# Batch 0's units reordered (tokens 0-255 first), and the mixing probabilities loaded later, in a retention + mixture-of-experts kernel

## The chip, the cores and the metric

The kernel runs on one core of one Trainium2 chip. The metric is device time in microseconds (us) of one execution. The profiled span is some 1.7 us shorter than the device time of the same execution. Runs that were sent together share one chip and one set of runs of the kernel before; sets 2 to 5 ran on four different chips (that of set 1 isn't on record), which turned out to matter.

## The reference, cut to what matters

```python
scores = scale * np.matmul(q, k.transpose(0, 1, 3, 2))        # B, H, S, D = 8, 8, 576, 64
ret    = scores * Dmat                                        # causal decay gamma_h ** (i - j)
attn   = np.matmul(ret, v)
x      = attn.transpose(0, 2, 1, 3).reshape(B * S, H * D)     # 4608 tokens x 512
p = domain_probs / (domain_probs.sum(-1, keepdims=True) + 1e-9)
for e in range(4):
    h = np.maximum(x @ w1[e], 0.0)                            # 512 -> 1024, "up"
    out += p[:, e:e + 1] * (h @ w2[e])                        # 1024 -> 512, "down"
```

Of the kernel before, what the change touches and what calls it, by code (L numbers as in the profile page):

```python
# [23 lines left out]
def kernel(  # L24
# [10 lines left out]
    nc = tc.nc  # L35
# [12 lines left out]
    NT = 512  # L48
# [50 lines left out]
    def load_w1(e, f=slice(0, F)):  # L99
        return nc.gpsimd.dma_start(out=w1_sb[e][:, :, f], in_=moe_w1[e][:, f].rearrange("(dc p) f -> p dc f", p=128))  # L100

    def load_w2(e):
        return nc.gpsimd.dma_start(
            out=wx[e // 2][:, (e % 2) * NFC:(e % 2 + 1) * NFC, :, :].rearrange("p a b c -> p a (b c)"),
            in_=moe_w2[e].rearrange("(fc p) d -> p fc d", p=128))
# [9 lines left out]
    def load_unit(raw, b, hf, g, eng):  # L115
        for n, src in srcs:
            eng.dma_start(out=raw[n],
                          in_=src[b, 4 * g:4 * g + 4, 2 * C * hf:2 * C * hf + 2 * C, :]
                          .rearrange("h (p r) d -> p h (r d)", r=2))

    units0 = ((0, 0), (1, 0), (0, 1), (1, 1))
    p0 = const.tile([128, NT // 128, E], FP32, name="p0")
    prb = tpool.tile([128, N // 128, E], FP32, tag="p1", name="prb")
    for u, (hf, g) in enumerate(units0):
        load_unit({n: raw0[u][n][:, :, :, :].rearrange("p h r d -> p h (r d)") for n in "kqv"}, 0, hf, g, nc.sync)
    nc.sync.dma_start(out=p0, in_=moe_domain_probs[0:NT, :].rearrange("(g p) e -> p g e", p=128))
    nc.sync.dma_start(out=prb, in_=moe_domain_probs.rearrange("(p t) e -> p t e", p=128))


    zz = epool.tile([128, 512], BF16)  # L130
# [41 lines left out]
    def later_tables():  # L172
        nc.gpsimd.memset(tri, 1.0)
        nc.gpsimd.affine_select(out=tri, in_=tri, compare_op=mybir.AluOpType.is_ge, fill=0.0,
                                base=0, channel_multiplier=-1, pattern=[[1, C]])
        nc.gpsimd.tensor_copy(trir[0:R], tri[0:R, 0:R])
        nc.gpsimd.tensor_copy(trir[R:2 * R], tri[R:2 * R, R:2 * R])
        nc.gpsimd.iota(pos_j[:, 0:NC], pattern=[[C, NC]], base=0, channel_multiplier=1,
                       allow_small_or_imprecise_dtypes=True)
        for j in range(2):  # L180
            nc.gpsimd.iota(pos_j[64 * j:64 * j + 64, NC:NC + 1], pattern=[[0, 1]], base=SM, channel_multiplier=1,
                           allow_small_or_imprecise_dtypes=True)
        for n in "kqv":
            nc.gpsimd.memset(rawr[n], 0.0)
# [23 lines left out]
    def mixing_weights():  # L208
        nc.vector.tensor_reduce(psm, prb, axis=mybir.AxisListType.X, op=ADD)
        nc.vector.tensor_scalar_add(psm, psm, 1e-9)  # L210
        nc.vector.reciprocal(psm, psm)
        nc.vector.tensor_tensor(pn, prb[:, :, :].rearrange("p t e -> p e t"),
                                psm.unsqueeze(1).to_broadcast([128, E, NTT]), op=MULT)
        nc.sync.dma_start(out=pd[:, :].rearrange("e (p t) -> p e t", p=128), in_=pn)
# [467 lines left out]
        if u + 1 < NU:  # L682
            us[u + 1].kv()
    part.matmuls(1)
    mixing_weights()
    early.close()
    hp = ctx.enter_context(tc.tile_pool(name="hp", bufs=1))
    h = hp.tile([128, E * NFC, NT], BF16, name="h")
# [25 lines left out]
        load_unit({n: raws[u][n].rearrange("p (h x) -> p h x", h=4) for n in "kqv"}, 1, vs[u].hf, vs[u].g, nc.gpsimd)  # L714

    load_w2(0)
    load_w1(1)
    later_tables()
    load_w2(1)
    load_rem(0, nc.gpsimd)  # L720
# [8 lines left out]
    def remainder(slots, b, at):  # L729
        add = lambda i, f: slots.setdefault(i, []).append(f)  # L730
        x = Rem(b)
        l, c, tr, s, o = at
        if b > 0:
            add(l, lambda: load_rem(b))
        add(c, lambda: x.cast(nc.vector))
        add(tr, x.trans_pe)
        add(s, x.scores)
        add(o, x.values)
# [4 lines left out]

    slots = {}
    add = lambda i, f: slots.setdefault(i, []).append(f)
    add(0, mixing_weights0)
    add(1, later_decays)
    remainder(slots, 0, (-1, 13, 15, 16, 17))

    def v_cast(u):  # L750
# [49 lines left out]
    for b in range(2, B):  # L800
        g = NS * (b - 3)
# [72 lines left out]
```

## The kernel before: what the change touches

The expert layer works on tiles of 512 tokens. Tile 0 can start when batch 0's attention is there, so batch 0 has a code of its own, the prologue here. It works in four units, each 256 tokens (`hf`) of four heads (`g`). Each unit is loaded, scaled and cast, transposed, and turned into scores, key-value state and values:

```python
units0 = ((0, 0), (1, 0), (0, 1), (1, 1))                     # (hf, g)
for u, (hf, g) in enumerate(units0):
    load_unit(..., 0, hf, g, nc.sync)                         # k, q, v: 256 KB each, SP queue
nc.sync.dma_start(out=p0, ...)                                # small table: tile 0's probabilities, 512 pieces of 16 B
nc.sync.dma_start(out=prb, ...)                               # large table: all of them, 72 KB
# ... casts; load_w1(0) in two halves after the casts of units 1 and 2, on the software queue ...
for u in range(NU):
    if u + 2 < NU:
        cast_unit(u + 2)
    if u == NU - 1:
        part = UpHalf(0)                                      # early up projection: tokens 0-255, half of expert 0
        part.matmuls(0)
    us[u].values_own()
    if u + 1 < NU:
        us[u + 1].scores()
    us[u].values_carried()                                    # 2 matmuls for hf 0, 4 for hf 1
    if u + 2 < NU:
        us[u + 2].trans_pe(1)
    if u + 1 < NU:
        us[u + 1].kv()                                        # 8 matmuls for hf 0, 12 for hf 1
part.matmuls(1)
mixing_weights()                                              # normalise prb, write it to DRAM
```

Behind it the weights are loaded on the software queue, and tile 0 goes through the experts. The calls in `slots` are run between its matmul groups:

```python
load_w2(0); load_w1(1); later_tables(); load_w2(1); ...       # 1 MB each, fp32 cast to bf16 on the way
slots: 0 mixing_weights0 (normalise p0), 1 later_decays, ...
for e in range(E):
    for i in range(4):
        if e > 0 or i > 1: up_group(h, 0, e, i)
        run(slots, n); n += 1
    for m in range(4):
        down_plain(h, 0, e, m); run(slots, n); n += 1         # the first reads load_w2(0)'s weights
```

PSUM is a ring of four buffers. `down_plain` fills one for two groups of 128 tokens, and VectorE scales it with the normalised probabilities.

## Time and profile before

| | kernel before |
|---|---|
| device time, median of the first 3 runs | 535.76 us (535.12 to 537.06) |
| TensorE busy | 526.5 us, 99% of the span |
| TensorE idle, 5-20 us | 1.29 us |
| early up projection starts | 18.09 us |
| first down weights land | 25.83 us |
| first down matmul starts | 25.95 us |

A row of the timeline has the start, the length, engine, line, operation, operands and count, and in brackets how long the engine was idle before and what ended it. A row of DMA issues has the size and the time from issue to landing. The lines are in the prediction below.

How to read the first down matmul: matmuls of 128x512 follow each other at a pitch of 0.216 us, and the up group before has 16 of them. So the first down matmul is due 16 x 0.216 = 3.46 us after that group's first one. What it comes later, it has waited.

### The profile page before, as it was taken

The page shows a single profiled execution, that of the slowest core. Times are in us where ns is not written, and L with a number is a line of the kernel's source. Part 1 is how long each engine was busy: PE and PEld are TensorE (multiplying, and loading weights), DVE is VectorE, ACT ScalarE, POOL GpSimd, SP SyncE. Part 2 cuts the span into 40 slices and gives each one's busy share as a digit, 9 for nine tenths or more (in the row PEclk, how much of TensorE's full clock was granted, in tenths as well). Part 3 has the DMA queues.
Part 4 walks back from the last instruction along what each step waited for, and adds up shares of the span by engine and source line. Part 5 has one row for each costly group of instructions (what it writes and reads, how often), then busy time and mean ns, then how long its engine had stood idle before and what let it go on. Part 6 is the DMA issues. An engine that isn't in the chain of part 4 may idle for free.

```text
span 533.7 us, 10229 instructions
## 1 busy us (share of the span) xinstructions
PE 526.5 (99%) x4260; PEld 342.4 (64%) x4260; DVE 361.7 (68%) x456; ACT 86.0 (16%) x175; POOL 144.5 (27%) x187
## 2 busy tenths in 40 slices
PE   8999999999999999999999999999999999999997
PEld 4644544478745885478646865587548844884486
DVE  6426668895577767697578767777765567557763
ACT  4723450012101121020101001100110000000010
POOL 5734104236235334335132603153000000000000
PEclk9999999999999999999999999999999999999999
DMA  9999947877879967937353655454010111110001
GB/s 240 205 213 250 239 114 190 165 156 168 143 168 166 174 138 145 158 81 167 101 135 95 152 134 112 107 120 124 20 41 21 60 39 41 41 41 20 1 21 60
DMA packets 145118, 63.55 MB, mean 119 GB/s; under 512 B 124240, under 2 KB 135888, under 8 KB 145072
## 3 DMA queue, kind: packets, MB, share of 16 engines
q1 hardware_dynamic: 134752, 43.50, 38.2%
q0 software_dynamic: 10176, 19.27, 16.4%
q8 instruction: 33, 0.54, 0.4%
q10 hardware_dynamic: 144, 0.13, 0.1%
q14 instruction: 13, 0.11, 0.1%
HBM read 53.56 MB, written 9.51 MB: 118 GB/s over the span
## 4 chain that ended last, share of the span: by engine, by line
PE 73%; ACT 2%; DVE 0%; issue 0%
PE ph L359 37%; PE pd L471 34%; ACT xt L292 2%; PE o L284 1%; PE o L279 1%; PE py L471 1%; DVE h L365 0%; PE sr L338 0%; PE or L344 0%; PE or L346 0%; DVE ob L499 0%
## 5 line engine op out<-in xcount | busy, mean ns | idle before, releaser
L359 PE MATMUL ph<-xt,w 128*128 128x512 bf16 x1136 | 251.0, 379 | 0.8 <-DVE h L365 0.2
L365 DVE SCALAR_TENSOR_TENSOR h<-ph,pB 128x1024 bf16<-128x1024 f32 x128 | 156.5, 1224 | 58.7 <-PE ph L359 58.0
L359 PEld LDWEIGHTS <-w 128*128 128x128 bf16 x1136 | 109.9, 98 | 127.9
L471 PEld LDWEIGHTS <-h 128*128 128x128 bf16 x1024 | 100.0, 98 | 13.3
L471 PEld LDWEIGHTS <-s 128*128 128x128 bf16 x768 | 75.0, 98 | 8.7
L471 PE MATMUL pd<-wx,h 128*128 128x256 bf16 x512 | 61.1, 273 | 0.2
L471 PE MATMUL pd<-wx,s 128*128 128x256 bf16 x512 | 61.1, 273 | 0.0
L220 POOL DMA_DIRECT2D pB<-pd x28 | 15.8, 565 | 150.9 <-DVE h L365 131.8
L506 POOL TENSOR_TENSOR ob<-v,p 128x256 f32<-128x256 f32 x15 | 11.3, 755 | 114.0 <-DVE v L503 92.5
L239 POOL TENSOR_TENSOR bf_k<-raw_k,gk 128x512 bf16<-128x512 f32 x24 | 25.8, 1073 | 35.3 <-DMA raw_k<-in_k_dram 17.4
L271 DVE TENSOR_TENSOR sT<-s,tri 128x1024 bf16<-128x1024 f32 x24 | 28.3, 1219 | 6.4 <-PE s L269 6.4
L292 ACT ACTIVATE xt<-o 128x768 bf16<-128x768 f32 (+6 forms) x24 | 13.0, 594 | 116.8 <-PE o L284 116.8
L444 DVE TENSOR_TENSOR s<-s,h 128x1024 bf16<-128x1024 bf16 x32 | 31.2, 1013 | 0.0
L471 PE MATMUL pd<-t4w,h 128*128 128x256 bf16 x256 | 30.6, 273 | 0.0
L394 PE MATMUL po<-wx,h 128*128 128x512 bf16 x128 | 29.1, 379 | 0.1
L471 PE MATMUL pd<-t3w,h 128*128 128x256 bf16 x240 | 28.7, 273 | 0.0
L471 PE MATMUL pd<-t2w,s 128*128 128x256 bf16 x240 | 28.6, 273 | 0.0
L479 ACT ACTIVATE p<-pd 128x256 f32<-128x256 f32 x16 | 6.1, 384 | 138.8 <-PE pd L471 106.2
L239 POOL TENSOR_TENSOR bf_q<-raw_q,gq 128x512 bf16<-128x512 f32 x24 | 26.9, 1120 | 3.3 <-DMA raw_q<-in_q_dram 3.1
L442 DVE TENSOR_TENSOR s<-h 128x1024 bf16<-128x1024 bf16 x32 | 24.8, 816 | 0.0
L448 DVE TENSOR_TENSOR s<-h,s 128x1024 bf16<-128x1024 bf16 x32 | 24.7, 811 | 0.0
L488 DVE TENSOR_TENSOR u<-pd,p 128x256 f32<-128x256 f32 x15 | 6.4, 425 | 22.5 <-PE pd L471 22.5
(158 smaller groups left out, 375.2 us busy)
## 6 DMA issues: line engine op xcount, KB each, us to landing
pB<-pd POOLq DMA_DIRECT2D x28, 256.0 KB, 3.7
raw_k<-in_k_dram SPq DMA_DIRECT2D x48, 128.0 KB, 2.8
raw_q<-in_q_dram SPq DMA_DIRECT2D x48, 128.0 KB, 3.0
raw_v<-in_v_dram SPq DMA_DIRECT2D x48, 128.0 KB, 3.0
wx<-in_moe_w_dram POOLq DMA_DIRECT2D x4, 1024.0 KB, 15.4
out_dram<-oa SPq DMA_DIRECT2D x16, 256.0 KB, 2.2
out_dram<-ob SPq DMA_DIRECT2D x15, 256.0 KB, 2.2
w<-in_moe_w_dram POOLq DMA_DIRECT2D x3, 1024.0 KB, 15.1
```

Of the source, the lines that this page charges most:

```text
L220: eng.dma_start(out=pB[t, e], in_=pd[e:e + 1, t * NT:(t + 1) * NT].to_broadcast([128, NT]))
L239: eng.tensor_tensor(bfs[p % 2][n], raw1[n], g[:, :, 2 * p:2 * p + 2].unsqueeze(3).to_broadcast([128, NC, 2, D]), op=MULT)
L271: nc.vector.tensor_tensor(sT[:, :, :, :].rearrange("p j c t -> p (j c) t"), s[:, :, :, :].rearrange("p j c t -> p (j c) t"), tri[:, :].uns ...
L292: nc.scalar.activation(xt_of(t)[:, self.ps, n0 + a - t * NT:n0 + z - t * NT], o[:, :, a:z], Copy)
L359: nc.tensor.matmul(ph[:, f, :], lhsT=w1_sb[e][:, dc, fc * 128:(fc + 1) * 128], rhs=x[:, dc, :], start=(dc == 0), stop=(dc == NDC - 1))
L365: nc.vector.scalar_tensor_tensor(h[:, fk:fk + 2, :], ph, 0.0, pB[t, e][:, :].unsqueeze(1).to_broadcast([128, 2, NT]), op0=MAX, op1=MULT)
L394: nc.tensor.matmul(po[:, g, :], lhsT=h[:, e * NFC + fc, ns * 128:(ns + 1) * 128], rhs=wx[e // 2][:, (e % 2) * NFC + fc, :, :].rearrange("p ...
L442: nc.vector.tensor_tensor(self.alloc("s1")[:, l], h[:, l, self.b], h[:, r, self.b], op=ADD)
L444: nc.vector.tensor_tensor(self.alloc("s2")[:, l], self.s1[:, l], h[:, l, self.a], op=SUB)
L448: nc.vector.tensor_tensor(self.alloc("s4")[:, l], h[:, r, self.a], self.s2[:, l], op=SUB)
L471: mm = nc.tensor.matmul(dst, lhsT=src[:, kk, tok], rhs=rhs(c), start=(start and c == 0), stop=(c == KH - 1), skip_group_check=True)
L506: nc.gpsimd.tensor_tensor(self.ob[:, HF:Dm], self.v, self.p5, op=ADD)
```

## The change

It has two aims: to let tokens 0-255 be done for all heads first, since the early up projection needs only those; and to keep the probability loads and their normalisation out of the stretch in which the first weights are loaded.

```diff
-    units0 = ((0, 0), (1, 0), (0, 1), (1, 1))
+    units0 = ((0, 0), (0, 1), (1, 0), (1, 1))
...
-    nc.sync.dma_start(out=p0, in_=moe_domain_probs[0:NT, :].rearrange("(g p) e -> p g e", p=128))
-    nc.sync.dma_start(out=prb, in_=moe_domain_probs.rearrange("(p t) e -> p t e", p=128))
...
     part.matmuls(1)
-    mixing_weights()
...
     load_w2(0)
+    nc.gpsimd.dma_start(out=p0, in_=moe_domain_probs[0:NT, :].rearrange("(g p) e -> p g e", p=128))
     load_w1(1)
+    nc.gpsimd.dma_start(out=prb, in_=moe_domain_probs.rearrange("(p t) e -> p t e", p=128))
...
-    add(0, mixing_weights0)
-    add(1, later_decays)
+    add(0, later_decays)
+    add(3, mixing_weights0)
+    add(9, mixing_weights)
```

## The prediction

> **What bounds the kernel now.** I read the page first: the busy shares, then the slices.
>
> ```profile
> span 533.7 us, 10229 instructions
> PE 526.5 (99%) x4260; PEld 342.4 (64%) x4260; DVE 361.7 (68%) x456; ACT 86.0 (16%) x175; POOL 144.5 (27%) x187
> ...
> DMA  9999947877879967937353655454010111110001
> ```
>
> TensorE is busy from the first slice to the last, so the end can only move if TensorE's program gets shorter or has fewer gaps. All of the change lies in the first 40 us (batch 0's attention, called the prologue here, and tile 0 of the expert layer), and there the DMA row is at 9 as well. Next I asked for the busy time by stretch, with the columns stretch, its length, PE busy, PEld, DVE, ACT, POOL, granted clock, DMA share, GB/s:
>
> ```profile
> 5.00:10.00 5.00, 4.57 (x48) 2.49 (x47) 2.95 (x4) 1.50 (x2) 1.50 (x3) 1.00 1.11 297
> 10.00:15.00 5.00, 4.64 (x104) 3.48 (x104) 4.65 (x7) 4.17 (x10) 2.51 (x5) 1.00 1.24 260
> 15.00:20.00 5.00, 4.50 (x88) 3.31 (x86) 3.47 (x9) 3.49 (x9) 4.62 (x13) 1.00 1.28 208
> 20.00:25.00 5.00, 5.00 (x36) 3.31 (x34) 1.56 (x19) 4.11 (x9) 3.82 (x6) 1.00 1.22 203
> 25.00:30.00 5.00, 4.94 (x24) 2.08 (x22) 0.40 (x1) 1.33 (x2) 0.77 (x1) 1.00 1.14 203
> ```
>
> Between 5 and 20 us PE is idle for 0.43 + 0.36 + 0.50 = 1.29 us in all, and afterwards hardly at all. This caps what can be won by filling gaps at something over 1 us of 534, far under 2%. The filler matmuls on a zero tile (20, of some 0.38 us) stay in the program where they are, so they can't be won. Then I read the timeline from 15 us to 26 us for what holds PE in the places the change touches (start, length, engine, line, operation, count, idle before it and its releaser):
>
> ```profile
> 16.08 0.76 ACT L598 ACTIVATE sbd<-kvp 64x256 bf16<-64x256 f32 x2
> ...
> 16.89 0.28 PE L623 MATMUL o<-qkT,sbd 128*128 128x128 bf16 x2 [0.24 <-ACT sbd L598]
> ...
> 17.01 1.15 PE L578 MATMUL kvp<-bf_v,bf_k 128*128 128x256 bf16 x12
> 17.21 0.77 ACT L639 ACTIVATE xt<-o 128x256 bf16<-128x256 f32 x2 [0.38 <-PE o L623]
> ...
> 18.09 1.05 PE L380 MATMUL ph<-xt,w 128*128 128x256 bf16 x8
> ...
> 22.27 3.62 PE L359 MATMUL ph<-xt,w 128*128 128x512 bf16 x16
> ...
> 25.91 6.60 PEld L394 LDWEIGHTS <-h 128*128 128x128 bf16 x32 [0.52 <-issue]
> ```
>
> L380 is the early up projection over tokens 0-255. It needs the third unit's xt, which ACT finishes at 17.21 + 0.77 = 17.98, and PE reaches it at 18.09 anyway because the key-value products before it run until then. L394 is the first down projection: its weight loads stood idle for 0.52 us, put down to "issue". The list of instructions says that this load also waits for a DMA of the software queue, the first down weights (wx). The DMA view for the moment of their issue at 14.93 us says:
>
> ```profile
> wx<-in_moe_w_dram POOLq DMA_DIRECT2D x1, 1024.0 KB, 10.9
> ```
>
> They land at 14.93 + 10.9 = 25.83, and PE goes on at 25.91. So this one wait of TensorE is for the DMA.
>
> **What the Trainium skill says.** "DMA: Bandwidth & Descriptors", section Issuing engines are not separate DMA queues: transfers started by different engines run on the same 16 DMA engines and interleave. The trace agrees. In the window 14.3-17.7 us the SP queue's probability loads took 22.5% of the engines' time, and the software queue moved 0.62 MB in 3.4 us (182 GB/s); in 17.7-19.2 us, alone, it moved 0.31 MB in 1.5 us (207 GB/s). The same page, Specifications: full rate wants at least 512 B a transfer. The trace agrees: 586 packets of the SP queue carried only 0.08 MB in that window. "Perfetto Trace Analysis", Identifying the Most-Contended Engine: matmul busy time doesn't tell the distance to the roofline. It agrees in so far as the 99% contain the 20 fillers; I use busy time only to find gaps.
>
> **The change part by part.** (1) Unit order. Before it was tokens 0-255 and 256-511 of heads 0-3, then the same of heads 4-7; now both head groups of tokens 0-255 come first. Loads, casts, transposes, scores, fillers keep number and size. A unit of tokens 256-511 has 12 key-value matmuls in place of 8, and 4 carried matmuls (L623) in place of 2. Before, units 2 and 4 had the long form; now 3 and 4 have. Unit 2 becomes shorter by 4 + 2 matmuls, where PE then waits for ACT: scores 3 follow ACT's qkT at 13.32 and the carried product follows ACT's sbd at 14.00, both as before. The gain is some 0.06 us (two fewer carried matmuls at some 0.06 us, of which one started before the wait). Unit 3 becomes longer: 4 more key-value matmuls, which fill the time to 15.95 in which PE waited for qkT (0.27 us idle before 16.23), and 2 more carried ones, one of them after the sbd of 16.84, 0.06 us more. In return, the early up projection's inputs are ready after unit 2 (about 15.2 in place of 17.98), but PE gets to it no sooner than 18.1, for unit 4's key-value products stand before it in the program. Here the intended release falls on a place where the wait had 0.1 us left. Sum of part 1: 0.0 us, give or take 0.15.
>
> (2) The probability loads leave the SP queue and go behind the first down weights. The software queue is then undisturbed: (207 - 182)/207 x 3.4 = 0.41 us sooner by 17.7. (3) Normalisation goes from before tile 0 to its slots 3 and 9. The write of the normalised table (issued 19.24, 528 packets in the window 22-28.6) no longer shares the engines: there the software queue moved 1.25 MB in 6.6 us, 189 GB/s, so 0.57 us are lost, some 0.33 of them before 25.83. The first down weights land 0.41 + 0.33 = 0.74 us sooner, near 25.1. PE gains only what it waited: the last of 16 L359 matmuls at a pitch of 0.216 us (32 in 7.07 us elsewhere) starts at 22.27 + 15 x 0.216 = 25.51, the next was due at 25.73 and came at 25.95, so 0.22 us. The vector work taken away before tile 0 (8 operations, 17.84-20.2 us) lay beside PE and gives nothing.
>
> What is added: two DMA issues on POOL, some 0.8 us each, before the second up weights (issue 15.81, now about 16.6; their bytes don't run until after 25 us), so nothing. The small table lands behind the down weights, by some 26.5 us; its four operations take about 1.0 us, and VectorE needs them for the first scaled output at 29.60: 2 us to spare. The large one needs to be in DRAM by the read at 74.64 us and, with normalisation near 36 us and 9.3 us of write, is there by about 47. VectorE is idle for 8.95 us before 43.41, so the 1.3 us of normalisation fit.
>
> Sum: -0.22 us, with 0.15 either way from part 1. 535.76 - 0.22 = 535.5; the before's median lies between 535.12 and 537.06, so I round to 535.5.
>
> **The rivals.** A: the small table comes late and VectorE holds PE through the PSUM ring. For it: 512 pieces of 16 B behind 1 MB on the software queue. Against: the ring has four buffers, and the first tile that needs a po buffer again is the third up group of expert 1, at 32.85 + 2 x 1.73 = 36.3; VectorE is done with that buffer at 31.0 now. The table would have to be over 5 us late beyond its 2 us of slack. It would make 536-538.
>
> B: PE comes sooner and waits for the second up weights instead. They land at 15.81 + 15.1 = 30.9, and PE loads them from 32.63: 1.7 us of slack, more than anything won here. Two loads more also shift the eight semaphores over which the software queue's transfers rotate, so that the third up weights are issued when the second have landed (about 30.7) in place of at 26.09. The second down weights, on their way until 19.70 + 16.6 = 36.3, keep the queue full, so no gap in the stream; were there one, PE would wait at 46 us and lose up to 4 us: 537-540.
>
> C: the token order is worth more than I find, since a chain of ACT and VectorE steps paces the units and may contract: at most the 1.29 us of idle PE, so 534.3.
>
> **Range and chances.** The central path gives 535.5. C and a larger effect of the DMA give 534.3, A or B in a mild form 536.8; the spread of three runs of one kernel is 1.9 us. I take 534.3 to 536.7 for 8 in 10. 2% is 10.7 us, which no part here can reach, as all that is touched has 1.5 us of idle time; slower by so much would need a stall of 10 us in tile 0. Chances: 0.01 faster, 0.98 the same, 0.01 slower.
>
> **What would show it right or wrong.** Right: the DMA view shows the first down weights landing in about 10.2 us in place of 10.9, the idle time before L394's first weight load shrinks from 0.52 to about 0.3, the first down matmul is at 25.7 in place of 25.95, the early up projection still starts at 18.0-18.2, and the timeline behind is the old one moved by 0.2 us. Part 1 is wrong if the early up projection starts before 17.9 or after 18.3. A shows as a wait of an up group near 36 us for VectorE, B as idle PE before 33 us or 46 us. The prediction as a whole is wrong if PE's idle time up to 60 us changes by over 1 us.

## The result, and the profile after

| | before | after |
|---|---|---|
| median | 535.51 us (535.12 to 537.06, 4 runs) | 535.24 us (535.14 to 536.35, 4 runs) |
| ratio | | 0.9994, 95% interval 0.997 to 1.0018 |

A ratio is the mean time of one kernel's fast runs over that of the other's of the same rounds, so it is not quite the ratio of the medians. The two kernels are the same within the noise.

The page of the changed kernel, the lines that answer to those of before:

```profile
span 533.5 us, 10230 instructions
...
PE 526.2 (99%) x4260; PEld 342.0 (64%) x4260; DVE 361.4 (68%) x456; ACT 85.9 (16%) x175; POOL 146.8 (28%) x189
```

Busy times by stretch (stretch, length, PE, PEld, DVE, ACT, POOL, granted clock, DMA share, GB/s):

```profile
10.00:15.00 5.00, 4.30 (x98) 3.02 (x99) 4.64 (x7) 4.22 (x10) 2.50 (x4) 1.00 1.19 257
15.00:20.00 5.00, 4.91 (x92) 3.79 (x90) 2.31 (x11) 3.43 (x9) 4.62 (x13) 1.00 1.21 185
20.00:25.00 5.00, 5.00 (x35) 3.24 (x34) 0.95 (x14) 4.11 (x9) 4.00 (x7) 1.00 1.21 201
25.00:30.00 5.00, 5.00 (x25) 2.17 (x24) 1.36 (x6) 1.28 (x2) 1.31 (x2) 1.00 1.14 216
```

TensorE's work has only moved: 0.34 us less in 10-15 us (4.64 to 4.30), 0.41 us more in 15-20 us (4.50 to 4.91); up to 60 us its busy time is 57.39 us before and 57.36 after. The long units now stand third and fourth. In the last row the 0.06 us of idle time before (4.94) is gone. The timeline of the changed kernel (its lines are 2 lower, so L378 is the early up projection and L392 the first down projection):

```profile
14.77 1.15 PE L576 MATMUL kvp<-bf_v,bf_k 128*128 128x256 bf16 x12
...
16.46 0.66 PE L621 MATMUL o<-qkT,sbd 128*128 128x128 bf16 x4
...
16.96 1.15 PE L576 MATMUL kvp<-bf_v,bf_k 128*128 128x256 bf16 x12
...
18.04 1.05 PE L378 MATMUL ph<-xt,w 128*128 128x256 bf16 x8
...
22.22 3.62 PE L357 MATMUL ph<-xt,w 128*128 128x512 bf16 x16
...
25.60 1.04 PEld L392 LDWEIGHTS <-h 128*128 128x128 bf16 x6 [0.25 <-issue]
25.68 7.07 PE L392 MATMUL po<-wx,h 128*128 128x512 bf16 x32
```

And the first down weights (wx), issued at 15.03 us, in the DMA view:

```profile
wx<-in_moe_w_dram POOLq DMA_DIRECT2D x1, 1024.0 KB, 10.5
```

The early up projection starts at 18.04 in place of 18.09. The first down matmul starts at 25.68, exactly when it is due (22.22 + 3.46), in place of 25.95. The span is 0.2 us shorter. In this one pair of traces it looks as predicted, but the weights landed at 15.03 + 10.5 = 25.53, not at 25.1. So the reasons had to be tested, and the first test was how much two traces of the same kernel differ.

### The profile page after: what moved, and what is told of

It is laid out like the page before. It is cut to its first block, busy times and chain, and to the rows that moved or that the text cites. A ratio compares the mean times of both kernels' runs of the same rounds, so it can differ in the third digit from the quotient of the medians.

```text
span 533.5 us, 10230 instructions
## 1 busy us (share of the span) xinstructions
PE 526.2 (99%) x4260; PEld 342.0 (64%) x4260; DVE 361.4 (68%) x456; ACT 85.9 (16%) x175; POOL 146.8 (28%) x189
## 4 chain that ended last, share of the span: by engine, by line
PE 73%; ACT 2%; DVE 0%; issue 0%
PE ph L357 37%; PE pd L469 34%; ACT xt L290 2%; PE o L282 1%; PE o L277 1%; PE py L469 1%; DVE h L363 0%; PE or L342 0%; PE sr L336 0%; PE or L344 0%; DVE ob L497 0%
## 5 line engine op out<-in xcount | busy, mean ns | idle before, releaser
L442 DVE TENSOR_TENSOR s<-s,h 128x1024 bf16<-128x1024 bf16 x32 | 29.9, 973 | 0.0
L392 PE MATMUL po<-wx,h 128*128 128x512 bf16 x128 | 29.1, 379 | 0.0
L446 DVE TENSOR_TENSOR s<-h,s 128x1024 bf16<-128x1024 bf16 x32 | 26.4, 863 | 0.0
L440 DVE TENSOR_TENSOR s<-h 128x1024 bf16<-128x1024 bf16 x32 | 23.7, 779 | 0.0
```

Of the source, the lines that this page charges most:

```text
L392: nc.tensor.matmul(po[:, g, :], lhsT=h[:, e * NFC + fc, ns * 128:(ns + 1) * 128], rhs=wx[e // 2][:, (e % 2) * NFC + fc, :, :].rearrange("p ...
L440: nc.vector.tensor_tensor(self.alloc("s1")[:, l], h[:, l, self.b], h[:, r, self.b], op=ADD)
L442: nc.vector.tensor_tensor(self.alloc("s2")[:, l], self.s1[:, l], h[:, l, self.a], op=SUB)
L446: nc.vector.tensor_tensor(self.alloc("s4")[:, l], h[:, r, self.a], self.s2[:, l], op=SUB)
```

## The experiments

My theory: the order is worth nothing, and moving the tables removes a wait of some 0.2 us for the first down weights, because the small table loads and the write of the table slow those weights. The main rivals: the order pays; or the landing of the weights moves by chance, and the tables have little to do with it.

All fourteen profiles, in us. "Due" is the up group's first matmul plus 3.46; "waited" is the start of the first down matmul less that. For the kernels with halves the landing is that of the first half. The last column is the span less the start of the first down matmul.

| run (set) | early up | first down weights land | first down starts | waited | span | span less start |
|---|---|---|---|---|---|---|
| before (1) | 18.09 | 25.83 | 25.95 | 0.22 | 533.7 | 507.75 |
| after (1) | 18.04 | 25.53 | 25.68 | 0.00 | 533.5 | 507.82 |
| before_again (2) | 18.04 | 25.54 | 25.72 | 0.04 | 533.4 | 507.68 |
| after_again (2) | 18.04 | 25.87 | 26.03 | 0.35 | 533.8 | 507.77 |
| order_only (2) | 18.10 | 25.25 | 25.73 | 0.00 | 533.4 | 507.67 |
| tables_only (2) | 18.25 | 25.15 | 25.88 | 0.00 | 533.7 | 507.82 |
| small_five (3) | 18.43 | 26.42 | 26.53 | 0.46 | 534.4 | 507.87 |
| tables_later (3) | 18.56 | 26.99 | 27.16 | 0.96 | 535.0 | 507.84 |
| tables_sp (3) | 18.48 | 25.66 | 26.11 | 0.00 | 533.8 | 507.69 |
| hoisted (3) | 17.50 | 25.08 | 26.65 | 0.00 | 534.5 | 507.85 |
| halves (4) | 17.76 | 21.77 | 25.39 | 0.00 | 533.2 | 507.81 |
| carry (4) | 17.37 | 24.99 | 25.12 | 0.11 | 533.0 | 507.88 |
| carry_halves (4) | 18.14 | 23.22 | 25.77 | 0.00 | 533.6 | 507.83 |
| carry_halves_again (5) | 17.44 | 23.36 | 25.07 | 0.00 | 532.9 | 507.83 |

The last column is the first finding. Whatever was changed, and on whatever chip, the span is the start of the first down matmul plus 507.67 to 507.88 us, while that start itself moves over 2.1 us. So in the profiled executions all that these kernels differ by lies before it, and it goes to the end undiminished. (The slowest executions, 537 to 542 us, were not profiled; where they lose their time isn't shown.)

### The two kernels once more

> The unchanged kernel once more, to see how far its landmarks in the trace move from one execution to the next. Ratio 1.000. Early up projection starts at 18.0-18.2 us, the first down weights land at 25.8 give or take 0.2, the first down matmul starts at 25.95 give or take 0.15.

> The changed kernel once more. Theory (the gain is the wait for the first down weights, 0.2 to 0.3 us): ratio 0.9995, the weights land at 25.5 give or take 0.2, first down matmul at 25.7. Rival (the two traces differ by chance in how fast the transfers ran): the weights land anywhere in 25.4-25.9 in both kernels, ratio 1.000.

Measured: before_again 535.60 us (ratio 1.0009, interval 0.9991 to 1.0028), after_again 535.38 us (1.0000, 0.9986 to 1.0014), the kernel before in the same rounds 535.45 us. The timeline of before_again:

```profile
25.68 0.99 PEld L394 LDWEIGHTS <-h 128*128 128x128 bf16 x6 [0.34 <-issue]
25.72 7.07 PE L394 MATMUL po<-wx,h 128*128 128x512 bf16 x32
```

and that of after_again:

```profile
26.00 6.60 PEld L392 LDWEIGHTS <-h 128*128 128x128 bf16 x32 [0.66 <-issue]
26.03 7.07 PE L392 MATMUL po<-wx,h 128*128 128x512 bf16 x32 [0.19 <-DMA wx<-in_moe_w_dram]
```

The roles are reversed, which fits the rival (landings anywhere in 25.4-25.9 in both kernels) and neither of my ranges for a landing: here it is the kernel before that hardly waits, and the changed one that waits 0.35 us, with the DMA named as the cause. The 0.27 us between the first two traces are no more than two traces of one kernel differ by. That the wait is for these weights stands; that the change removes it does not.

### One part of the change at a time

```diff
 order_only: the kernel before with
-    units0 = ((0, 0), (1, 0), (0, 1), (1, 1))
+    units0 = ((0, 0), (0, 1), (1, 0), (1, 1))
 tables_only: the changed kernel with that line taken back
```

> Kernel before with the unit order alone changed. Theory (order is worth nothing to within 0.1 us, since the early up projection stands behind the last unit's key-value products): early up projection at 18.0-18.2, down weights still land at 25.8, first down matmul still at 25.9-26.0, ratio 1.000. Rival (the order is what pays): early up projection before 17.9, first down matmul before 25.8, ratio 0.9995.

> Changed kernel with the unit order of before. Theory: the down weights land at 25.5, the first down matmul starts at 25.7-25.75, ratio 0.9995 as for the whole change. Rival (order pays): weights sooner, but first down matmul at 25.75 or later and ratio 1.000.

Measured: order_only 535.60 us, ratio 1.0011 (0.9994 to 1.0027); tables_only 535.44 us, 1.0015 (0.9991 to 1.0039). The first unit's key-value products and the early up projection of order_only, in the timeline:

```profile
9.34 0.71 PE L578 MATMUL kvp<-bf_v,bf_k 128*128 128x128 bf16 x8
...
16.51 0.67 PE L623 MATMUL o<-qkT,sbd 128*128 128x128 bf16 x4
17.02 1.15 PE L578 MATMUL kvp<-bf_v,bf_k 128*128 128x256 bf16 x12
18.10 1.05 PE L380 MATMUL ph<-xt,w 128*128 128x256 bf16 x8
```

The order alone leaves it at 18.10, directly behind the last unit's key-value products. This is as predicted. tables_only, though, came out as the rival (the order pays) had forecast: weights sooner, at 25.15, but the first down matmul at 25.88. The traces settle it. From the start of the first unit's key-value products to the early up projection it is 18.10 - 9.34 = 8.76 us in order_only, 18.25 - 9.49 = 8.76 in tables_only and 18.09 - 9.33 = 8.76 in the kernel before, and 8.76 or 8.77 in all ten profiles that change nothing in this part of the program but the order: four with the old order and six with the new. So the order is worth nothing to within 0.01 us, and the rival that it pays is refuted. tables_only was 0.15 us later than order_only already at the first unit's products. These start between 9.00 and 10.00 us in the fourteen profiles; the latest is carry_halves, whose second unit's query load took 6.0 us in place of 4.7 to 5.8.

But order_only's weights landed at 25.25 with the tables still in their old place, earlier than in either trace of the whole change, so a landing time alone doesn't tell where the tables were. The times can't separate any of this.

### Four more loads of the small table

```diff
 kernel before, after the two table loads:
+    p0x = const.tile([128, 4, NT // 128, E], FP32, name="p0x")
+    for i in range(4):
+        nc.sync.dma_start(out=p0x[:, i], in_=moe_domain_probs[0:NT, :].rearrange("(g p) e -> p g e", p=128))
```

> Kernel before with the small table loaded five times over on the SP queue (four more loads of 512 pieces of 16 B, into a tile that nobody reads), a dose of the suspected cost. Theory (each such load takes some 0.35 us from the weights' stream): the first down weights land at about 27.0 in place of 25.7, first down matmul at 27.0, end 1.2 us later, ratio 1.0023. Rival (the small pieces overlap with the stream and cost nothing, what differs from execution to execution is chance): weights land within 25.2-25.9, ratio 1.000.

Measured: 536.28 us against 536.09 for the kernel before on this chip, ratio 1.0000 (0.9986 to 1.0015). Chips and executions differ in when the first loads arrive, so I count from the landing of the last attention load. From there to the landing of the down weights it is 11.73 us with the dose. In the three profiles with the tables in the old place and no dose it was 11.49, 11.64 and 10.78, on average 11.30. So four loads cost some 0.4 us, 0.1 us each, which is less than the spread of 0.86 us between those three. The 0.35 us a load that I expected would have made it 12.7 us. The bytes are clearer than the landings. In 14.3-17.7 us the software queue moved 0.56 MB with the dose, against 0.62 to 0.63 in those three profiles (the SP queue took 34.3% of the engines' time in place of 21.2 to 22.5%), and in 17.7-22 us 0.84 against 0.88. At the 207 GB/s that the prediction reads for the undisturbed stream, these 0.10 MB are an estimated 0.5 us. So in this one trace the loads do slow the stream, by about a third of what I took.

### The tables in other late places

```diff
 tables_later: the changed kernel with both table loads behind load_w1(1)
 tables_sp: the changed kernel with both loads back on the SP queue, but held back:
+    def late(t, src):
+        nc.vector.memset(t, 0.0)
+        nc.sync.dma_start(out=t, in_=src)
+    add(2, lambda: late(p0, ...)); add(5, lambda: late(prb, ...))
```

> Changed kernel with both table loads behind the second up weights instead of one behind the first down weights. Theory (VectorE's late start costs TensorE nothing before some 36 us): the small table lands at 30.6, VectorE's first scaling of an output starts near 31.8 in place of 29.3, TensorE's third up group of expert 1 doesn't wait, ratio to the kernel before 0.9995-1.000. Rival A of the prediction (VectorE holds TensorE through the PSUM ring): a TensorE wait near 36 us, 0.5-2 us, ratio 1.001-1.004. If the small table behind the first down weights slows those, they land sooner here, at 25.0-25.2.

> Changed kernel with the table loads off the software queue again, on the SP queue but only when the first down weights are in (held back by a fill of the table on VectorE, at about 24.8 and 30.7 us). Theory (the software stream was slowed at 18-21 us by the loads put on its queue, which took back what their leaving the SP queue gave): no such slow stretch, first down weights land at 25.0-25.2, first down matmul at 25.7 in every execution, median 535.1, ratio 0.9993. Rival (the slow stretch has another cause): weights at 25.4-25.9 as in the changed kernel, median 535.4.

Measured: tables_later 535.68 us, ratio 0.9993 (0.9976 to 1.0011); tables_sp 535.46 us, 0.9994 (0.9973 to 1.0015). The timeline of tables_later and its list of TensorE's waits from 14 to 60 us:

```profile
33.13 2.73 DVE L402 TENSOR_SCALAR acc<-po,pm 128x512 f32<-128x512 f32 x4
```

```profile
PE po L392 <- DMA wx<-in_moe_w_dram: 0.8, 1, 0.8
PE o L621 <- ACT sbd L596: 0.2, 1, 0.2
```

VectorE scaled the first output at 33.13, 3.8 us later than in the changed kernel (29.33), and at 33.52 in tables_sp. TensorE didn't wait for it in either. So rival A of the prediction (VectorE holds TensorE through the PSUM ring) is refuted well beyond the delay that the change could cause. The 0.8 us wait is for the weights: in this execution the last attention load took 6.2 us in place of 5.1-5.3, and the down weights behind it were issued 1 us late, at 16.39 (15.46 in tables_sp on the same chip). This is one source of the spread between executions.

tables_sp was also to show what took back the gain of the first trace. The software queue's bytes by stretch, first in the kernel before (14.3-17.7, then 17.7-22 us):

```profile
q0 software_dynamic: 622, 0.62, 109.4%
...
q0 software_dynamic: 878, 0.88, 123.4%
```

then in the changed kernel:

```profile
q0 software_dynamic: 686, 0.68, 123.5%
...
q0 software_dynamic: 759, 0.77, 118.7%
```

and in tables_sp:

```profile
q0 software_dynamic: 678, 0.68, 121.4%
...
q0 software_dynamic: 769, 0.77, 118.8%
```

The columns are packets, MB and share. With the tables out of the way the stream moved 0.06 MB more by 17.7 us, in the direction predicted, and 0.11 MB less in the next 4.3 us. The first of these holds throughout: 0.62 to 0.63 MB in the three profiles with the tables in the old place, 0.56 with the dose, and 0.65 to 0.69 in all ten with the tables moved. So that the table loads take from the stream in this stretch is shown; in the first trace it loses 0.06 MB while the SP queue moves 0.08 MB. I had blamed the table loads on the same queue. In tables_sp none was under way then, and the slow stretch is there all the same, with the landing at 25.66 in the rival's range (25.4-25.9), so that cause falls. All six profiles of sets 1 to 3 with the tables moved have it (0.66 to 0.83 MB in that stretch, against 0.88 in the three with the tables in the old place and no dose), and none of the four of sets 4 and 5 (0.87 to 0.88 MB), which have the tables moved as well and ran on other chips; carry's loads are those of the changed kernel. What slows the stream there stays open.

### The early up projection moved forward

```diff
 changed kernel:
-        if u == NU - 1:
-            part = UpHalf(0)
-            part.matmuls(0)
...
             us[u + 2].trans_pe(1)
+        if u == NU - 2:
+            part = UpHalf(0)
+            part.matmuls(0)
         if u + 1 < NU:
             us[u + 1].kv()
```

> Changed kernel with the first part of the early up projection moved ahead of the last unit's key-value products, so that the new order's early inputs can be used. Theory (order frees the inputs at 15.1, but the first half of the up weights lands only at 17.0-17.7): TensorE idles from 16.9 to the landing, the last unit comes some 1.0-1.6 us later, the up stage after it 0.5-1.2 us later, ratio 1.001-1.002. Rival (the order pays once the program uses it): early up projection starts at 16.9, first down matmul no later than 25.7, ratio 0.999-1.000.

Measured: 536.43 us, ratio 1.0000 (0.9985 to 1.0016). The timeline:

```profile
17.50 1.05 PE L378 MATMUL ph<-xt,w 128*128 128x256 bf16 x8 [0.34 <-DMA w<-in_moe_w_dram]
18.39 1.15 PE L576 MATMUL kvp<-bf_v,bf_k 128*128 128x256 bf16 x12
...
20.39 0.34 PE L621 MATMUL o<-qkT,sbd 128*128 128x128 bf16 x3 [0.35 <-ACT sbd L596]
```

The new order does have the inputs ready early, but the first half of the up weights lands at 9.80 + 7.7 = 17.50, and TensorE waits for it by name. The last unit then comes late, and the first down matmul starts at 26.65, late by its own program and not for want of weights. The median is 0.3 us over the kernel before; the interval doesn't settle that, the trace does. The order can't pay here because the next input isn't there.

### Two changes that follow from this

If the time is set by when the first down matmul starts, there are two ways to make it sooner: do away with the wait for the down weights, and take work from TensorE ahead of it. `halves` loads expert 0's down weights as two halves and does its down projection in two passes. `carry` drops the repeated key-value products of tokens 0-255 and adds the stored state instead:

```diff
 halves (changed kernel):
-    load_w2(0)
+    load_w2_half(0, 0)
+    load_w2_half(0, 1)
...
+        if e == 0:
+            for m in range(4):
+                down_plain(h, 0, e, m, range(NFC // 2))
         for m in range(4):
-            down_plain(h, 0, e, m)
+            down_plain(h, 0, e, m, range(NFC // 2, NFC) if e == 0 else range(NFC))
 carry (changed kernel):
-            if hf == 1 and self.carry is None:
-                for g in range(2):
-                    mm(g, 128, slice(0, 2), 0)
...
+                if hf == 1 and self.carry is None:
+                    nc.vector.tensor_tensor(dst, src, sbd[jr, gs, 1, jr].unsqueeze(2).to_broadcast([64, 2, 2, D]), op=ADD)
...
 carry_halves: both
```

> Changed kernel with the first down weights loaded in two halves, and expert 0's down projection in two passes over them (same matmuls, other order), so that TensorE needs only the first half at first. Theory (the wait for these weights is all that differs from execution to execution in the prologue): first half lands 2.5 us sooner than the whole did, near 23, no wait at the first down matmul, which stands at the pitch of 0.216 us after the up group in every profile (3.46 us after its first matmul); median near the lowest times of the kernel before on the same chip, ratio 0.9993. Rival (the wait costs nothing, something behind takes it back): same first down start, span no longer than 507.75 us behind it, ratio 1.000.

> Changed kernel with 8 key-value matmuls less before the early up projection: units of tokens 256-511 take the products of tokens 0-255 from the stored state (an addition on VectorE in place of a copy on ScalarE) and don't repeat them. Theory (TensorE's work sets the early up projection, the landing of the weights sets the first down matmul): early up projection 0.4 us sooner, near 17.6, or when the first half of the up weights lands, 17.2-17.7; but first down matmul not before the landing at 25.2-25.9, so ratio 0.999-1.000. Rival (weights don't bind): first down matmul at 25.2-25.3, end 0.45 us sooner, ratio 0.9990.

> Both of the last two. Theory: early up projection near 17.6, first down matmul 0.4-0.5 us sooner than without wait before, near 25.25 (later by as much as this chip's first loads are later), end 0.5-0.8 us sooner than the kernel before, ratio 0.9988, no wait of TensorE for weights in tile 0. Rival (the second up weights, landing near 30.5, bind next): TensorE waits before 32.0.

> The last kernel once more, since the profile of it fell on an execution whose first loads came about 1 us late (first half of the up weights issued at 10.49 in place of 9.2-9.5). Theory: with loads in time, early up projection at the landing of the first up weights or near 17.5, first down matmul 3.45 us after the up group before it and so near 25.0-25.3, span 507.8 us behind it, median 0.4-0.7 us under the kernel before, ratio 0.9985-0.9995. Rival (the gain of the last job was chance): median and ratio as the kernel before.

Measured, all with correct results:

| run | median | kernel before, same rounds | ratio, 95% interval |
|---|---|---|---|
| halves | 535.28 | 535.59 | 0.9976 (0.9936 to 1.0015) |
| carry | 534.92 | 535.59 | 0.9973 (0.9933 to 1.0013) |
| carry_halves | 535.13 | 535.59 | 0.9974 (0.9934 to 1.0015) |
| carry_halves_again | 534.77 | 535.55 | 0.9987 (0.9975 to 0.9999) |

In set 4 the kernel before had two executions of 538.15 and 542.0 us, which make its mean and so these three ratios look better than they are; there I go by the medians. They are 0.3 to 0.7 us under the kernel before, but each of the three intervals includes 1; four of carry's five executions are faster than all eleven of the kernel before. The timeline of carry:

```profile
25.09 0.99 PEld L392 LDWEIGHTS <-h 128*128 128x128 bf16 x6 [0.42 <-issue]
25.12 7.07 PE L392 MATMUL po<-wx,h 128*128 128x512 bf16 x32
```

The weight load sits idle until 25.09, just behind the landing at 24.99: with less work ahead, TensorE runs into the wait for the down weights, though these landed early enough here that it cost only 0.11 us. The timeline of carry_halves_again:

```profile
17.44 1.05 PE L384 MATMUL ph<-xt,w 128*128 128x256 bf16 x8 [0.24 <-DMA w<-in_moe_w_dram]
...
24.86 6.79 PEld L398 LDWEIGHTS <-h 128*128 128x128 bf16 x32
25.07 7.07 PE L398 MATMUL po<-wx,h 128*128 128x512 bf16 x32
```

Here the down weights don't bind at all: the weight load has no idle time before it, and the first half landed at 23.36. What binds now is the first half of the up weights, by name, at 17.44. Five of its six executions are faster than all eleven of the kernel before; its interval is the only one that lies under 1. It beats the kernel before by 0.13%; the changed kernel was not run beside it. The first profile of this kernel showed no gain, because it fell on an execution with late loads (early up at 18.14). Counted from the first unit's key-value products, the early up projection came after 8.19 us in carry and 8.14 in carry_halves, in place of 8.76: the work taken away is worth some 0.6 us there, where I expected 0.4. In carry_halves_again it is 8.41, with the wait of 0.24 us for the up weights. What the halves add to carry, these times don't show.

## Why the prediction was right or wrong

The time was right: 535.5 forecast, 535.24 measured, the same within 2%, inside the range. The forecast gain of 0.22 us can neither be confirmed nor refuted by times whose intervals are 0.14 to 0.24% (0.8 to 1.3 us) wide on either side. That the first pair of traces differed by about the forecast amount (0.2 us in the span) was luck.

- **Where the end is set** (the early part of TensorE's program, passed on undiminished): right, and shown fourteen times over by the constant 507.7-507.9 us.
- **Part 1, the order, 0.0 give or take 0.15 us**: right, and rival C, that the order is worth more, falls with it. 18.04-18.10 with the new order against 18.04-18.25 with the old in sets 1 and 2, and 8.76 us after the first unit's key-value products with both; the last unit's key-value products are what stands before it. hoisted added what I hadn't seen: the up weights land at 17.5, so the order couldn't have paid much even with the program changed.
- **Part 2 and 3, "The first down weights land 0.41 + 0.33 = 0.74 us sooner, near 25.1"**: this is the step that failed. With both parts they landed at 25.53 and 25.87, without at 25.83 and 25.54, and took 10.5 and 10.8 us from issue to landing, not 10.2, against 10.9 and 11.0. The averages of the landings are the same, but the stream of before_again started early (issue at 14.54 in place of 14.93-15.07). Counted from the landing of the last attention load it is 11.13 and 11.45 with both parts, 11.49 and 11.64 without; over sets 1 to 3 10.96 on average in the six profiles with the tables moved and 11.30 in the three without move or dose. So the sum was 0.74 and measures some 0.3, and the ranges (10.54 to 11.45, 10.78 to 11.64) overlap. The first term is borne out in direction: the 0.06 MB more by 17.7 us are an estimated 0.3 us at 207 GB/s, where I took 0.41. What the prediction lacked is the slow stretch at 17.7-22 us in sets 1 to 3, which cost the stream 0.05 to 0.22 MB, for a reason left open. The 0.33 us for the write of the table was never tested alone.
- **"PE gains only what it waited ... 0.22 us"**: the mechanism is right (after_again names the DMA), but the size was one draw: in the unmodified program the wait was 0.22 in one execution and 0.04 in another, in the changed one 0.00 and 0.35. I should have treated a single trace's 0.2 us as such.
- **What is added costs nothing**: right. The small table landed at 15.90 + 9.8 = 25.70, VectorE scaled at 29.33, and delays of some 4 us more (rival A) cost TensorE nothing.
- **Rival B, the shifted semaphores**: the third up weights were issued at 30.71, as forecast (30.7), and TensorE had no wait for the second or third up weights up to 60 us in either profile of the changed kernel.

## What to carry to other kernels

Before explaining a few tenths of a microsecond by two traces, profile each of the two kernels twice: here one pair showed the forecast gain and the other showed its reverse. In a stretch where TensorE is full and the first transfers just keep up, making inputs ready earlier gives nothing unless the next input (here the weights) is there too, and trimming work gives only what the next landing allows. A constant distance between two landmarks, or from one to the end, is a quick test of where variants really differ: here the 8.76 us show in every trace that the order is worth nothing, which no run's time could. Compare landings from a landmark too, since the loads before them start at different times.

## What the Trainium skill lacked or had wrong

- "DMA: Bandwidth & Descriptors" says that transfers of small pieces are slow themselves, but gives no figure for what they take from a large stream on the same engines. Here, beside 2048 more pieces of 16 B, the weights' stream moved 0.56 MB in 14.3-17.7 us in place of 0.62 to 0.63, and 0.84 in place of 0.88 in 17.7-22 us. The 1 MB load landed 11.73 us after the last attention load in place of 11.30 on average, a difference smaller than the spread (10.78 to 11.64).
- The same page gives no spread between executions of one program. Here the landing of the same 1 MB load differed by 0.3 us between two executions (25.83 and 25.54; 25.53 and 25.87), and the last attention load, of 256 KB, took 5.1 to 5.3 us in all profiles but one, where it took 6.2 and the first down matmul then waited 0.96 us.
